# Moving weight block sums, range tests, the verdict and the last products of a gated-recurrence-plus-ELU-layer kernel

## The chip, the cores and the metric

The program runs on one core of one Trainium2 chip. The metric is the device time of one execution in microseconds. Five engines of the core matter: TensorE (PE in the profile), VectorE (DVE), ScalarE (ACT), GpSimd (POOL) and SyncE (SP), which here only issues DMAs. Each engine takes its own instructions strictly in the order in which the program lists them, and waits at an instruction until what it needs is there.

## The reference

```python
# attention block: q, k, v, a_re, a_im are (4, 8, 768, 48), float32
mag = np.sqrt(a_re * a_re + a_im * a_im)
scale = np.minimum(mag, 0.999) / (mag + 1e-06)
a_re_n, a_im_n = (a_re * scale, a_im * scale)
for t in range(S):
    ar, ai = (a_re_n[:, :, t, :, None], a_im_n[:, :, t, :, None])
    new_re = ar * S_re - ai * S_im
    new_im = ar * S_im + ai * S_re
    kv = np.einsum('bhd,bhe->bhde', k[:, :, t], v[:, :, t])
    S_re, S_im = (new_re + kv, new_im)
    y[:, :, t] = np.einsum('bhd,bhde->bhe', q[:, :, t], S_re)
# bridge: (B,H,S,D) -> (B*S, H*D) = (3072, 384) = x
h = x @ w_in                                  # (384, 2048)
g = np.where(h > 0.0, h, np.exp(np.minimum(h, 0.0)) - 1.0)
out = g @ w_out                               # (2048, 384)
```

A complex gated linear recurrence runs over 768 steps for 32 heads; its output is the input of a two-layer network with an ELU between the layers. The two weight matrices arrive as float64 and are read by the kernel as pairs of 32-bit words.

## The kernel before

**Units.** The work is cut into `NU = 12` units. A unit is 128 time steps of two batches (256 rows of the network). Two chains of batches alternate, so unit `u` hands its state and its phase to unit `u + 2`. Each unit has an attention half and a layer half.

**The attention half** works with logarithms and angles of the gates instead of stepping through time. The functions that matter here, with their lines, are: `squares` and `joined` (L709, L710, L716), `logarithms` and `powers` (L735 to L747), `lengths` (L772, reads tile `e` and is the last to do so), `ratios` (L759, L760), `slopes` (L780, the last reader of tile `w` before the carry), `angles` (L815), `carried` (L826), `turned` (matmul L837, then L842 and L845 on VectorE), `waves` (L973 to L977), `scaled` (L982 on GpSimd for k, L992 on VectorE for q) and `gated` (L1003). `carried` adds the phase that unit `u - 2` ended with to row 0 of the angles; `carry_back` (L820, a DMA on GpSimd's queue) fetches that row from DRAM into row 0 of a tile that is free by then, and `carry_on` (L862) has stored it there. `turned`'s matmul sums the angles over time, so it cannot start before `carried`. `noted` (L796, L799) reduces the gates to their least and greatest values and is the last reader of the tiles `ar` and `ai`, which have one buffer each. `states`, `scored` and `valued` (L1064 to L1145) form the attention products, and `quartered` (L889) the sums of logarithms. `seam` (L1190, six small DMAs on GpSimd's queue) moves parts of the result into the layer's input `x`.

**The layer half** of units 0 to 2 is plain (`hidden`, L1210 to L1221). From unit 3 on the first layer is a block scheme with fewer products: `mixed` (L1410) and `mixed_rest` (L1430) form sums of input blocks, and `mult` (L1450) multiplies 20 of them, in the order `ORDER = 8, 1, 6, 3, 9, 7, 5, 0, 2, 14, 12, ...`, with 20 weight blocks into five PSUM banks; `kept` (ACT, L1463) and `joint` (DVE, L1466) combine the banks, `low` (L1471, L1472) and `whole_of` (L1475) do the ELU. The second layer is a block scheme too: `folded` (DVE, L1297) prepares operands, and `product` (L1319) makes seven products P1 to P7, each in two halves `h`. When a product's second half is there, `done` inside `product` combines it (L1331, L1332, L1341 on DVE, L1339 on ACT) into an output tile `o`, which has two buffers, and issues the DMA to DRAM.

**Weight block sums.** The blocks that the schemes multiply with are sums and differences of the weights. They are made once, in place or in spare tiles, by `summed_in` (L1398, L1400; 21 of them in the list `SUMS`, each 128x512) and `combined` (L1278; eight of them, 128x768), while unit 2's plain layer still runs. Unit 3 is the first that needs them.

**Range tests.** The fast path is valid only for weights and gates in a certain range. `test_fetch` (L666, L669) loads one of `NR = 48` pieces of the raw weights into one buffer (the last quarter of `spare[1]`), `test` (L680) reduces it on VectorE. There is one such buffer, so a fetch waits for the test before it. `verdict` (L1483 to L1502) combines all of this into the flag `needs` with a matmul (L1499); at the end every engine reads the flag and skips a slow general path.

**The order** of everything is written out by hand. `first` lists the opening; after it, `put(at, fn, ...)` gives each step a place in slots, 16 slots to a unit (one unit takes about 50 us in the trace), and all steps are issued in the order of these places:

```python
    for n in range(len(SUMS)):
        put(37 + 0.6 * n if n < 11 else 45.4 + 0.6 * (n - 11), summed_in, n)
    ...
    for m in range(NR):
        put(54 + 2.5 * m, test_fetch, m)
        put(56 + 2.5 * m, test)
    put(NU * SLOTS, verdict)
```

The layer of unit `u` has its `mult`s at `16 (u - 2) + 36` and its products at `+ 44`. So between slots 45 and 53 lie, together, unit 2's products, unit 4's gates with `carried(4)` at 48.6, and the sums that unit 3's `mult`s from slot 52 on will read.

Of the kernel before, what the change touches and what calls it, by code (L numbers as in the profile page):

```python
# [505 lines left out]
def kernel(  # L506
# [179 lines left out]
    def flat(t):  # L686
        return t.rearrange("p n h d -> p (n h d)")
# [5 lines left out]
    def new(tag, bufs=1, shape=None):  # L693
        return sb.tile(shape or [C, NB, H, D], FP32, tag=tag, bufs=bufs, name=tag)
# [122 lines left out]
    def carry_back(u):  # L817

        if u in carry and u > 3:
            nc.gpsimd.dma_start(out=flat(nat[u]["w"])[0:1], in_=carry[u])  # L820

    def carried(u):

        if u in carry:
            row = nat[u]["th"][0:1].rearrange("p n h d -> p (n h d)")
            nc.vector.scalar_tensor_tensor(  # L826
                out=row, in0=carry[u] if u < 4 else flat(nat[u]["w"])[0:1], scalar=float(2 * np.pi), in1=row, op0=ALU.mult,
                op1=ALU.add,
            )

# [468 lines left out]
    def product(u, k, h):  # L1299

        x = nat[u]
        bank, n, first = {
            1: (0, 0, True), 2: (0, 0, False), 6: (0, 1, False), 5: (1, 0, True),
            7: (1, 1, False), 3: (0, 0, True), 4: (2, 0, True),
        }[k]
        if first and h == 0 and k != 3:
            x["p", bank] = work([C, 2, HN], "mlp")
        to = x["p", bank][:, n]
        a = {
            1: lambda: X(u, h, 0, 0), 2: lambda: X(u, h, 0, 1), 3: lambda: S_of(u, 4, h),  # L1310
            4: lambda: X(u, h, 1, 1), 5: lambda: S_of(u, 1, h), 6: lambda: S_of(u, 2, h),
            7: lambda: S_of(u, 3, h),
        }[k]()
        if k < 4:
            b = Y(*((0, 0), (1, 0), (1, 1))[k - 1])[:, ts(h, P // 2)]
        else:
            b = T_of({4: 4, 5: 1, 6: 2, 7: 3}[k], h)
        for m in range(P // 2):
            nc.tensor.matmul(  # L1319
                to, lhsT=a[:, m], rhs=b[:, m], start=(first and h == 0 and m == 0), stop=False,  # L1320
                skip_group_check=True,
            )
        if h == 0 or k in (4, 5):
            return
        if k == 1:
            x["u"] = new("ee", 2, [C, 2, GT])
            nc.scalar.copy(out=x["u"][:, 0, 0:HN], in_=to)
            return
        u2, u4 = (x["u"][:, n, 0:HN] for n in range(2))
        if k == 6:  # L1330
            nc.vector.tensor_tensor(out=u2, in0=to, in1=u2, op=ALU.add)  # L1331
            nc.vector.tensor_tensor(out=u4, in0=x["p", 1][:, 0], in1=u2, op=ALU.add)  # L1332
            return
        seq, at = where(u)

        def done(i, n, a, *sums):
            o = new("o", 2, [C, HN])
            if not sums:
                nc.scalar.copy(out=o, in_=a)  # L1339
            for b, op in sums:  # L1340
                nc.vector.tensor_tensor(out=o, in0=a, in1=b, op=op)  # L1341
                a = o
            nc.sync.dma_start(out=out[ds((seq + i) * S + at, C), ts(n, HN)], in_=o)

        if k == 7:
            done(1, 1, to, (u4, ALU.add))
            done(1, 0, to, (u2, ALU.add), (x["p", 2][:, 0], ALU.subtract))
        elif k == 2:
            done(0, 0, to)
        else:  # L1350
            done(0, 1, to, (u4, ALU.add))
# [13 lines left out]

    def A(r, k):

        if r == "e":
            return spare[0][:, ts(k, 4 * C)] if k < 4 else (
                more[:, k - 4] if k < 7 else spare[1][:, ds(8 * C, 4 * C)]  # L1370
            )
        h, j = ROLES[r]
        return w_in[:, k].rearrange("p (h m j f) -> p h j m f", h=2, j=2, f=C)[:, h, j]

    def four(t):
        return t.rearrange("p (m f) -> p m f", f=C) if len(t.shape) == 2 else t
# [11 lines left out]
        (17, (0, 1), PLUS, (2, 1)), (15, (0, 2), MINUS, (0, 0)), (12, 15, NEITHER, 17),  # L1388
        (17, 17, PLUS, (1, 1)), (17, 17, MINUS, 16), (2, (1, 1), MINUS, 12),
        (13, (1, 0), MINUS, 2), (11, (1, 0), MINUS, 10),  # L1390
    ] + SUMS[11:]

    def summed_in(n):

# [49 lines left out]
    def mult(u, p):  # L1444

        x = nat[u]
        c = next(c for c in BANKS if p in BANKS[c])
        a = four(A(*IN_OF[p]))
        for m in range(4):
            nc.tensor.matmul(  # L1450
                x["c" + c][:, ts(m, C)], lhsT=a[:, m], rhs=x["mix"][p],
                start=(p == BANKS[c][0] and m == 0), stop=False, skip_group_check=True,
            )
# [26 lines left out]
    def verdict():  # L1480

        ones, fit = value(1.0, "ones"), seen[:, 0 : NU + NR]
        nc.vector.tensor_tensor(  # L1483
            out=off[:, :, 0], in0=off[:, :, 0], in1=off[:, :, 1], op=ALU.add
        )
        nc.vector.tensor_scalar(
            out=least, in0=least, scalar1=LEAST_RE, scalar2=None, op0=ALU.is_ge
        )
        nc.vector.scalar_tensor_tensor(
            out=least, in0=most, scalar=LEAST_RE, in1=least, op0=ALU.is_le, op1=ALU.mult  # L1490
        )
        nc.vector.tensor_scalar(
            out=least[:, 0:OFF], in0=off[:, :, 0], scalar1=0.0, scalar2=None, op0=ALU.is_le
        )
        nc.vector.tensor_scalar(
            out=smallest, in0=smallest, scalar1=LEAST_HI, scalar2=None, op0=ALU.is_ge
        )
        t = work([1, NU + NR])
        nc.tensor.matmul(t, lhsT=ones, rhs=fit, start=True, stop=True)  # L1499
        n = cst.tile([1, 1], FP32, name="n")  # L1500
        nc.vector.tensor_reduce(out=n, in_=t, axis=mybir.AxisListType.X, op=ALU.add)
        nc.vector.tensor_scalar(  # L1502
            out=needs, in0=n, scalar1=C * (NU + NR) - 0.5, scalar2=None, op0=ALU.is_lt
        )
# [57 lines left out]
    def decays_of(u, *at):  # L1562
        fns = squares, joined, logarithms, powers, lengths, ratios, slopes, noted, angles, carried
        if u > 3:
            put(at[6] + 0.3, carry_back, u)
        put(at[0], begun, u)
        for x, fn in zip(at, fns):
            put(x, fn, u)
# [60 lines left out]
    def layer_of(u, at_h, at_p):  # L1629
# [5 lines left out]
        else:  # L1635
# [24 lines left out]
            put(at_h + 0.4 * 17.6, folded, u, 0, (3, 1))  # L1660
            put(at_h + 0.4 * 22, folded, u, 1, (3, 1))
        ks = [(k, h) for k in (1, 4, 2, 5, 6, 7, 3) for h in range(2)]
        step = 8 / len(ks)
        for m, (k, h) in enumerate(ks):
            put(at_p + m * step, product, u, k, h)
# [4 lines left out]
    for u in range(2, NU):  # L1670
        r = (u - 2) * SLOTS
        put(r + (8 if u == PAIRED else 4.5 if u == PAIRED + 3 else 1.5), load_a, u)
        put(r + 8, load_v, u)
        put(r + 8, load_qk, u)
        if u == 2:
            decays_of(u, 16, 16, 17, 17, 18.4, 19.5, 19.6, 22.7, 19.8, 19.8)
            gates_of(u, 20.4, 21.6, 22.1, 22.4, 22.4, 22.6)
        else:
            sq = (r + 7.2, r + 9.6) if u < PAIRED + 4 else (r + 5.08, r + 6)
            noting = r + (15.7 if u != PAIRED + 2 else 20.3)  # L1680
            decays_of(u, *sq, r + 12.8, r + 13.2, r + 13.4, r + 13.5, r + 14.9, noting, r + 15.52, r + 16.6)
            gates_of(u, r + 15, r + 17.2, r + 17.4, r + 18.6, r + 18)
            put(r + 18.7, gated, u, None, ("q",))
            put(r + 18.8, gated, u, None, ("k",))
            if u > PAIRED + 1:
                put(r + (19.45 if u < PAIRED + 4 else 21.1), table, "exp_and_others", u)
                put(r + 15.5, table, "trig_and_small", u)
            if u > PAIRED + 1:
                put(r + 16.8, scaled, u, "k", None)
        if u > PAIRED:  # L1690
            for n in range(NB):
                put(r + 22 + 2 * n, transposed, u, "q", n)
                put(r + 23 + 2.3 * n, transposed, u, "k", n)
            at = r + (31.3 if u + 1 < NU else 30.6)
            put(r + 28.2, scored, u)
            put(at, valued, u)
            put(at, seam, u)
            put(r + 34.45, mixed, u)
            put(r + 34.75, mixed_rest, u)
        layer_of(u, r + 36, r + 44)  # L1700
    for n in range(len(SUMS)):
        put(37 + 0.6 * n if n < 11 else 45.4 + 0.6 * (n - 11), summed_in, n)
    for m, x in enumerate(((1, 0), (2, 0), (1, 1), (4, 0), (2, 1), (4, 1), (3, 0), (3, 1))):
        put(37.2 + m * 0.6 if m < 6 else 40 + m, combined, *x)
    for m in range(NR):
        put(54 + 2.5 * m, test_fetch, m)
        put(56 + 2.5 * m, test)
    put(NU * SLOTS, verdict)
    items = [(fn, tuple(args)) for fn, *args in first]
    items += [x[2:] for x in sorted(plan, key=lambda x: x[:2]) if x[2:] not in items]  # L1710
    for fn, args in items:
# [37 lines left out]
```

## Time and profile before

| | us |
|---|---|
| median of 3 runs | 679.25 (678.58 to 681.2) |
| the profiled execution's own time | 677.98 |
| its span, first to last instruction | 676.2 |
| TensorE busy | 642.4 (95%) |
| VectorE busy | 502.3 (74%) |
| ScalarE busy | 419.1 (62%) |
| GpSimd busy | 157.8 (23%) |
| mean granted TensorE clock | 0.986 of full speed |

The page of the profile gives busy shares per engine and in 40 slices of 16.9 us. The list of waits says which engine waited for which, in us in total, times and longest. The timeline shows the instructions of one engine in order, with start, duration, and in brackets how long the engine stood idle before and what ended that. The 1.8 us between the span and the execution's own time are start and end outside the instructions.

### The profile page before, as it was taken

Reading aid. Unit: us, or ns where it says so; the run is one execution under the profiler, and the core shown is the slowest. Engines: PE = TensorE matmul, PEld = TensorE weight load, DVE = VectorE, ACT = ScalarE, POOL = GpSimd, SP = SyncE. Lnnn points to the kernel's source line nnn. Section 1 sums busy time; section 2 is a strip of 40 time slices with the busy share of each in tenths; the row PEclk is TensorE's granted clock in tenths of the full one; section 3 lists DMA queues with packets and bytes.
Section 4 is the critical chain, followed back from the end, with each engine's and each line's share of the span. In section 5 each row is a group of like instructions: output and inputs, shape, how many; then the busy total and the mean of one; then the engine's idle time right before and its main releaser. Section 6 shows DMA issues by size and latency. Waiting matters only on the chain.

```text
span 676.2 us, 17220 instructions
## 1 busy us (share of the span) xinstructions
PE 642.4 (95%) x7236; PEld 581.7 (86%) x7236; DVE 502.3 (74%) x800; ACT 419.1 (62%) x684; POOL 157.8 (23%) x200
## 2 busy tenths in 40 slices
PE   8899899999997999999999999999999999999995
PEld 6777785577896998998998998998998998999994
DVE  5889999957759678778778778778678777664481
ACT  6875455865854577677677677667677667571350
POOL 2000000122123313503503503504503503402000
PEclk9799999999998999999999999999999999999998
DMA  9995755531900452352441722441642351210000
GB/s 168 175 159 99 144 173 164 82 72 20 153 3 14 93 91 67 77 116 57 102 88 40 147 58 72 104 87 43 116 86 68 75 116 31 66 33 13 18 7 24
DMA packets 151443, 56.12 MB, mean 83 GB/s; under 512 B 129684, under 2 KB 143164, under 8 KB 151356
## 3 DMA queue, kind: packets, MB, share of 16 engines
q1 hardware_dynamic: 147616, 53.58, 39.1%
q0 software_dynamic: 3520, 1.20, 1.8%
q8 instruction: 59, 0.97, 0.6%
q14 instruction: 28, 0.23, 0.1%
q10 hardware_dynamic: 220, 0.14, 0.1%
HBM read 48.91 MB, written 4.80 MB: 79 GB/s over the span
## 4 chain that ended last, share of the span: by engine, by line
PE 53%; DVE 11%; ACT 9%; issue 4%; DMA 2%; SPq 0%; DVEq 0%; ACTq 0%
PE mlp L1319 18%; PE mlp L1450 9%; PE y L1450 6%; PE w L1023 4%; PE mlp L1210 3%; PE w L1064 3%; PE y L1109 3%; DVE g L1466 2%; PE w L837 2%; PE y L1136 2%; DVE g L1475 2%; PE mlp L1235 2%; ACT L735 2%; ACT n L746 1%; DVE g L1297 1%
## 5 line engine op out<-in xcount | busy, mean ns | idle before, releaser
L1319 PE MATMUL mlp<-w_out,g 128*128 128x192 f32 x640 | 113.3, 331 | 1.8 <-DVE ee L1332 1.8
L1319 PEld LDWEIGHTS mlp<-w_out,g 128*128 128x128 f32 x640 | 105.9, 192 | 5.5 <-DVE ee L1332 2.4
L1081 POOL TENSOR_TENSOR S<-S,T 128x384 f32<-128x384 f32 x36 | 33.6, 932 | 178.3 <-DVE S L1079 178.3
L1210 PE MATMUL mlp<-x,w_in 128*128 128x256 f32 x288 | 65.1, 381 | 2.7 <-DVE g L1221 2.4
L1210 PEld LDWEIGHTS mlp<-x,w_in 128*128 128x128 f32 x288 | 53.8, 190 | 11.3 <-DVE g L1221 2.8
L1297 DVE TENSOR_TENSOR g<-g 128x512 f32<-128x512 f32 x80 | 57.7, 731 | 5.0 <-PE mlp L1319 3.8
L1466 DVE TENSOR_TENSOR g<-g,mlp 128x512 f32<-128x512 f32 x45 | 30.7, 683 | 38.2 <-PE mlp L1450 23.9
L1450 PE MATMUL mlp<-x,w_in 128*128 128x128 f32 x432 | 57.2, 275 | 0.0
L1319 PE MATMUL mlp<-w,g 128*128 128x192 f32 x320 | 54.7, 329 | 0.0
L1475 DVE SCALAR_TENSOR_TENSOR g<-ee,g 128x512 f32<-128x512 f32 x63 | 44.1, 700 | 12.2 <-ACT ee L1472 11.9
L1450 PEld LDWEIGHTS mlp<-x,w_in 128*128 128x128 f32 x432 | 52.6, 192 | 0.0
L1319 PEld LDWEIGHTS mlp<-w,g 128*128 128x128 f32 x320 | 51.8, 190 | 0.7
L1471 ACT ACTIVATE ee<-g 128x512 f32<-128x512 f32 x63 | 39.5, 627 | 19.5 <-DVE g L1466 19.3
L1463 ACT COPY g<-mlp 128x512 f32<-128x512 f32 x36 | 21.2, 588 | 43.4 <-PE mlp L1450 43.2
L1472 ACT ACTIVATE ee<-ee 128x512 f32<-128x512 f32 x72 | 45.4, 631 | 2.3
L1190 POOL DMA_DIRECT2D x<-y x62 | 30.1, 493 | 59.4 <-ACT y L1126 37.5
L973 ACT ACTIVATE cs<-n 128x768 f32<-128x768 f32 (+1 forms) x14 | 10.5, 750 | 43.1 <-DVE n L845 43.1
L1024 ACT COPY qt<-w 128x512 f32<-128x512 f32 x48 | 25.8, 589 | 16.0 <-PE w L1023 15.9
L904 ACT ACTIVATE n<-w 64x384 f32<-64x384 f32 (+1 forms) x60 | 28.1, 486 | 8.9 <-PE w L889 8.3
L1450 PE MATMUL y<-x,w_in 128*128 128x128 f32 x216 | 29.3, 278 | 4.0 <-ACT g L1463 4.0
L1450 PEld LDWEIGHTS y<-x,w_in 128*128 128x128 f32 x216 | 26.2, 192 | 4.9 <-ACT g L1463 4.8
L1219 ACT ACTIVATE ee<-mlp 128x512 f32<-128x512 f32 x24 | 14.3, 595 | 25.6 <-PE mlp L1210 16.8
(218 smaller groups left out, 1436.8 us busy)
## 6 DMA issues: line engine op xcount, KB each, us to landing
w<-in_moe_w_out_dram SPq DMA_DIRECT2D x8, 768.0 KB, 4.4
g<-in_moe_w_in_dram SPq DMA_DIRECT2D x24, 256.0 KB, 3.0
g<-in_moe_w_out_dram SPq DMA_DIRECT2D x24, 256.0 KB, 2.9
w<-in_moe_w_in_dram SPq DMA_DIRECT2D x16, 288.0 KB, 5.7
vn<-in_v_dram SPq DMA_DIRECT2D x24, 192.0 KB, 3.9
out_dram<-o SPq DMA_DIRECT2D x48, 96.0 KB, 2.2
ar<-in_a_re_dram SPq DMA_DIRECT2D x22, 192.0 KB, 3.6
ai<-in_a_im_dram SPq DMA_DIRECT2D x22, 192.0 KB, 4.3
```

The costliest lines, as they stand in the source:

```text
L904: nc.scalar.activation(out=flat(x[key][to, n : n + 1]), in_=t[of], func=AF.Exp, scale=sign)
L1023: nc.tensor.transpose(t[:, h], of, ident)
L1081: eng.tensor_tensor(out=new_s, in0=new_s, in1=wide, op=ALU.mult)
L1190: eng.dma_start(out=x["x"][ds(j * HP + D, G), i], in_=x["y"][ds(j * HP + i * G, G)])
L1210: nc.tensor.matmul(t[:, e], lhsT=w_in[:, i, ts(f + e, C)], rhs=x["x"][:, i], start=(i == 0), stop=(i == NI - 1),)
L1297: nc.vector.tensor_tensor(out=S_of(u, k, h), in0=a, in1=b, op=op)
L1319: nc.tensor.matmul(to, lhsT=a[:, m], rhs=b[:, m], start=(first and h == 0 and m == 0), stop=False, skip_group_check=True,)
L1450: nc.tensor.matmul(x["c" + c][:, ts(m, C)], lhsT=a[:, m], rhs=x["mix"][p], start=(p == BANKS[c][0] and m == 0), stop=False, skip_group_che ...
L1466: nc.vector.tensor_tensor(out=part(u, to), in0=part(u, a), in1=part(u, b), op=op)
L1471: nc.scalar.activation(out=e, in_=part(u, of), func=AF.Relu, scale=-1.0)
L1472: nc.scalar.activation(out=e, in_=e, func=AF.Exp, scale=-1.0)
L1475: nc.vector.scalar_tensor_tensor(out=part(u, to), in0=nat[u]["e", to], scalar=-1.0, in1=part(u, of), op0=ALU.add, op1=ALU.max,)
```

## The change

Six edits, all of them in where steps stand or which buffer they use:

1. The 21 sums get places one by one. The first 11 stay. Of the other ten, one (index 20) stays ahead of `carried(4)` and nine go behind it, from slot 49.3 to 59.5, among unit 3's layer. A new 22nd sum makes block 6 a second time, in the still unused test buffer, ahead of the carry (slot 45); unit 3's `mult` of block 6 reads that copy, so that the sum in place (index 19) can come after unit 3's layer. Two `combined` steps move from slots 46 and 47 to 40.8 and 41.4.
2. `carry_back` goes from after `slopes` to after `lengths`, into tile `e` instead of tile `w`.
3. `noted(4)` moves from slot 52.3 to 49.6.
4. The 48 tests stand at six fixed places in each unit instead of every 2.5 slots, and each fetch comes right behind the test before it.
5. `verdict` moves 7.5 slots forward and is cut in two; the part that reads the matmul's result, `pronounced`, comes 2.5 slots later.
6. In the last two units the last four product halves go (3, h0), (7, h0), (7, h1), (3, h1) instead of (7, h0), (7, h1), (3, h0), (3, h1). The last unit's four output tiles are taken from the ring `S` (eight buffers) instead of the ring `o` (two).

```diff
     def carry_back(u):
         if u in carry and u > 3:
-            nc.gpsimd.dma_start(out=flat(nat[u]["w"])[0:1], in_=carry[u])
+            nc.gpsimd.dma_start(out=flat(nat[u]["e"])[0:1], in_=carry[u])
...
-                out=row, in0=carry[u] if u < 4 else flat(nat[u]["w"])[0:1], scalar=float(2 * np.pi), in1=row, op0=ALU.mult,
+                out=row, in0=carry[u] if u < 4 else flat(nat[u]["e"])[0:1], scalar=float(2 * np.pi), in1=row, op0=ALU.mult,
...
         def done(i, n, a, *sums):
-            o = new("o", 2, [C, HN])
+            if u < NU - 1:
+                o = new("o", 2, [C, HN])
+            else:
+                o = flat(new("S", 8, [C, 1, H, D]))[:, 0:HN]
...
     def A(r, k):
+        if r == "t":
+            return spare[1][:, ds(12 * C, 4 * C)]
...
-    ] + SUMS[11:]
+    ] + SUMS[11:] + [(("t", 0), (1, 1), MINUS, 5)]
...
-        a = four(A(*IN_OF[p]))
+        a = four(A(*(("t", 0) if p == 6 and u == PAIRED + 1 else IN_OF[p])))
...
-        t = work([1, NU + NR])
+        nat[0]["fit"] = t = work([1, NU + NR])
         nc.tensor.matmul(t, lhsT=ones, rhs=fit, start=True, stop=True)
+    def pronounced():
+        t = nat[0]["fit"]
...
         if u > 3:
-            put(at[6] + 0.3, carry_back, u)
+            put(at[4] + 0.05, carry_back, u)
...
         ks = [(k, h) for k in (1, 4, 2, 5, 6, 7, 3) for h in range(2)]
+        if u > NU - 3:
+            ks[-4:] = (3, 0), (7, 0), (7, 1), (3, 1)
...
-            noting = r + (15.7 if u != PAIRED + 2 else 20.3)
+            noting = r + (15.7 if u != PAIRED + 2 else 17.6)
...
-    for n in range(len(SUMS)):
-        put(37 + 0.6 * n if n < 11 else 45.4 + 0.6 * (n - 11), summed_in, n)
+    for n in range(11):
+        put(37 + 0.6 * n, summed_in, n)
+    for n, at in (
+        (21, 45), (20, 46.5), (11, 49.3), (12, 49.4), (13, 49.5), (16, 50.2), (14, 54.3),
+        (15, 55.1), (17, 56), (18, 57), (19, 59.5),
+    ):
+        put(at, summed_in, n)
...
-        put(37.2 + m * 0.6 if m < 6 else 40 + m, combined, *x)
+        put(37.2 + m * 0.6, combined, *x)
+    clear = [SLOTS * n + x for n in range(3, NU) for x in (0.55, 5.2, 7.35, 9.7, 12.3, 14.2)]
+    clear = [x for x in clear if x > 57]
     for m in range(NR):
-        put(54 + 2.5 * m, test_fetch, m)
-        put(56 + 2.5 * m, test)
-    put(NU * SLOTS, verdict)
+        put(clear[m - 1] + 0.01 if m else 55, test_fetch, m)
+        put(clear[m], test)
+    put(NU * SLOTS - 7.5, verdict)
+    put(NU * SLOTS - 5, pronounced)
```

More of the change, by code (lines that the diff above doesn't have):

```diff
@@ L1700 @@
         layer_of(u, r + 36, r + 44)
-    for n in range(len(SUMS)):
-        put(37 + 0.6 * n if n < 11 else 45.4 + 0.6 * (n - 11), summed_in, n)
+    for n in range(11):
[5 more added lines that the diff above has]
+        put(at, summed_in, n)
     for m, x in enumerate(((1, 0), (2, 0), (1, 1), (4, 0), (2, 1), (4, 1), (3, 0), (3, 1))):
-        put(37.2 + m * 0.6 if m < 6 else 40 + m, combined, *x)
+        put(37.2 + m * 0.6, combined, *x)
+    clear = [SLOTS * n + x for n in range(3, NU) for x in (0.55, 5.2, 7.35, 9.7, 12.3, 14.2)]
+    clear = [x for x in clear if x > 57]
     for m in range(NR):
-        put(54 + 2.5 * m, test_fetch, m)
-        put(56 + 2.5 * m, test)
-    put(NU * SLOTS, verdict)
+        put(clear[m - 1] + 0.01 if m else 55, test_fetch, m)
+        put(clear[m], test)
+    assert clear[NR - 1] < NU * SLOTS - 8
+    put(NU * SLOTS - 7.5, verdict)
+    put(NU * SLOTS - 5, pronounced)
     items = [(fn, tuple(args)) for fn, *args in first]
```

## The prediction

> **What bounds the kernel now.** First the page's slices (40 of 16.9 us each, digits are tenths):
>
> ```profile
> PE   8899899999997999999999999999999999999995
> ...
> DVE  5889999957759678778778778778678777664481
> ...
> PEclk9799999999998999999999999999999999999998
> ```
>
> TensorE is the bound: nine tenths or more in nearly every slice. The exception after the opening is the 13th slice (203 to 220 us), where TensorE falls to 7, VectorE stands at 9 and the clock then dips. So the question is what TensorE waits for. The waits, longest first:
>
> ```profile
> PE w L837 <- DVE n L826: 4.3, 1, 4.3
> PE y L1450 <- ACT g L1463: 4.0, 4, 1.8
> ...
> PE w L889 <- DVE n L772: 2.0, 8, 0.3
> PE mlp L1319 <- DVE ee L1332: 1.8, 2, 0.9
> ```
>
> One wait of 4.3 us for the carry, four of 4.0 us together in the `mult`s, eight of a quarter microsecond (0.25 each, paced by ScalarE's table loads; no edit touches them). The timeline shows the long one, and beside it the same steps four units' worth later, undisturbed:
>
> ```profile
> 215.00 2.90 PE L837 MATMUL w<-n,sum_turns 128*128 128x384 f32 x4 [4.31 <-DVE n L826]
> 217.69 6.90 PE L1319 MATMUL mlp<-w_out,g 128*128 128x192 f32 x32
> ...
> 371.74 1.53 PE L837 MATMUL w<-n,sum_turns 128*128 128x384 f32 x4
> 373.11 5.36 PE L1319 MATMUL mlp<-w_out,g 128*128 128x192 f32 x32
> ```
>
> TensorE idles 4.31 us, and then the same matmuls take nearly twice as long: from 215.00 to the first `mult` at 224.43 are 9.43 us, from 371.74 to 378.31 6.57 us. That is another 2.86 us. Why `carried` (L826) was late, and what it met:
>
> ```profile
> 212.24 2.62 DVE L826 SCALAR_TENSOR_TENSOR n<-n 1x768 f32<-1x768 f32 x1
> ...
> 212.22 1.81 POOL L982 TENSOR_TENSOR k<-k,n 128x768 f32<-128x768 f32 x1
> ...
> 370.65 0.95 DVE L826 SCALAR_TENSOR_TENSOR n<-n 1x768 f32<-1x768 f32 x1 [0.35 <-ACT n L815]
> ```
>
> VectorE is busy without a gap from 201.48, with six sums and two `combined` between `lengths` and `carried`, and reaches L826 at 212.24, though ScalarE had its angles ready at 209.65. There it starts 13 ns after GpSimd's L982 and takes 2.62 us instead of 0.95.
>
> The `mult` waits come from tests that stand too close to the one before; the single buffer makes each wait out a whole transfer:
>
> ```profile
> 588.52 0.42 DVE L680 TENSOR_REDUCE seen<-g 128x1 f32<-128x256 f32 x1 [3.45 <-DMA g<-in_moe_w_out_dram]
> ...
> 592.36 1.16 PE L1450 MATMUL y<-x,w_in 128*128 128x128 f32 x8 [1.11 <-ACT g L1463]
> ...
> 669.93 0.36 DVE L1341 TENSOR_TENSOR o<-mlp,ee 128x192 f32<-128x192 f32 x1 [2.35 <-DMA out_dram<-o]
> ```
>
> VectorE stands at the test, so `joint` is late, so ScalarE's `kept` is late, so TensorE waits. The last line is the tail: the final output tile waits for an earlier one's DMA, since `o` has two buffers.
>
> [...] the clock stands at one half for 6.83 us from 213.97 (6.83/2 = 3.4 us lost, 2.86 of them before the first `mult`), and no later gap (1.78 us at most) does it. [...] 2.62 us is L982's rest, 1.80, and L826's own 0.95 less overlap. [...] the tests' transfers here, from SP, take 2.6 us at least, 2.9 to 3.0 in the median and 4.8 at most, which I use.
>
> **The change, part by part.** Signs are of time; negative is a gain.
>
> *Sums and carry (edits 1 and 2).* VectorE's costs from start to start in the trace: 0.60 us for a 128x512 sum, 0.87 for a 128x768 step. In the changed order only two sums (the copy of block 6, which stands in VectorE's 3.55 us idle before L772, and one more) remain ahead. From 201.48: L772, L759, L760 (0.87 + 0.98 + 0.87), one L1297, one sum, L780, two L1297 end at about 207.5. L826 then waits for ScalarE alone, until 209.65, as it does at 370.65. GpSimd: `seam`'s six DMAs cannot start before ScalarE's L1180 ends (207.5) and take 2.88 us, so L982 starts at about 210.4, with L826 under way. `carry_back`'s DMA, now after L772 at 202.4, has 7 us for a landing of 2.1. So L837 starts at 210.7, where TensorE gets there: **-4.31, and -2.86 of half clock.** The two `combined` (2 x 0.87) fall into VectorE's idle stretches of 1.3 to 1.6 us ahead of L1221 around 186: 0.
>
> *What is late next.* The four sums placed at 49.3 to 50.2 and the two reductions of `noted(4)` stand between L845 and `done`'s L1341: 4 x 0.60 + 2 x 0.87 = 4.1 us. In the undisturbed unit VectorE has 1.04 us idle there. So L1341 comes 3.0 us later than the undisturbed place: at 217.9 instead of 214.9. The first `mult` needs a PSUM bank that the second L1341 frees (0.62 later, 218.5), where TensorE would be ready at 217.3: 1.3 us. The second `mult` needs `halves`, the second L1410, 1.8 us after the first L1341: another 0.3. The sixth needs the bank read by the fourth L1341, 6.15 us after the first, 224.0, where TensorE would be at 223.3: 0.7. **+2.3.** [...] The sums at 54.3 to 57 (4 x 0.60) lie where VectorE waits 2 to 3 us for TensorE in each unit: 0[...]. The last sum stands in the dense end of the ELU chain: 0.60, less a test that left: **+0.3.** All readers come after the sums, by more than 5 us.
>
> *`noted(4)` earlier (edit 3).* It frees `ai` sooner; SP then issues unit 5's loads behind the last output of unit 2, at about 224.5 instead of 229.8. The 1.78 us gap at 237.19 had 0.44 us of waiting for that load on ScalarE; the rest is `squares(5)` itself standing ahead of `kept`. **-0.45.**
>
> *Tests (edit 4).* 48 x 0.33 us before and after. Between tests there are now 4.1 us at least (slots 14.2 to 16.55: L780, one L1297, L796, L799, one L1297), else 6 or more, against transfers of 2.9 to 3.0. SP has nothing before these fetches that waits. The loads of v, q, k move 6 us behind a fetch; they are read 25 us later. The three other `mult` gaps go: **-0.15, -0.99, -1.11.**
>
> *Verdict (edit 5).* Five small steps (0.74 us from 657.29 to 658.03) fall into 2.07 us of idle VectorE at 641; the matmul's 0.2 us only moves. L1501 and L1502 (0.31) now stand in the chain that product P4 waits for (0.53 us at 651.51): **+0.3.**
>
> *Last products (edit 6).* P7 waits for L1332, twice, 0.91 us; P3 instead waits only for L1331, which ends 0.38 earlier, and covers L1332: **-0.76.** In the tail the last L1341 follows the last matmul (669.13) at 669.2 instead of 669.93: **-0.7.**
>
> Sum: -7.17 + 2.3 + 0.3 - 0.45 - 2.25 + 0.3 - 0.76 - 0.7 = **-8.4 us.** Against the profiled 677.98 that is 669.6. The median is 1.3 above that execution, so I forecast 679.25 - 8.4 = **670.8.**
>
> **Bounds.** The wait ahead of `mult` is not in the trace before: between 0 (then 668.5) and 3.0 plus a half-clock stretch of 3.4 (then 674.9); I take the reckoned 2.3. The half clock may not be lost in every timed run[...]: up to +2.9. The rest of the 1.78 gap may go: -1.3.
>
> **Rivals.** *A. The queue is shifted, not removed.* The sums hold up the `mult`s for 3 us and the clock falls again: 670.8 + 0.7 + 3.4 = 674.9. For it: VectorE is as full there as before the carry. Against: three short gaps[...]. *B. No half clock in the timed runs, and the fixed tests wait as the old ones did:* 670.8 + 2.9 + 2.25 = 676.0, no difference. Against: 4.1 us of distance is more than the median landing. *C, slower: the test ahead of the carry.* In units 5 to 11 a test stands right ahead of `carried`, its fetch 3.7 us earlier. If the piece lands later than that plus 0.4 us, L826 falls behind GpSimd's L982[...], and L837 is late by some 2.5 us in each unit: 7 x 2.5 = 17.5, 670.8 + 17.5 = 688. It decides from a landing of 4.1 us; for slower by over 0.5% ((8.4 + 3.4)/2.5) five of the seven must fail. For it: one transfer took 4.8. Against: the median is 3.0, and the w_out pieces never took over 3.1. *D. No wait ahead of `mult`, all else as reckoned:* 668.5.
>
> **Chances.** Forecast 0.63 (its own range 668.5 to 673), A 0.17, B 0.09, C 0.04, D 0.07. A measurement here can tell about 0.5%, 3.4 us, from no change: below 675.9 is faster. Faster 0.63 + 0.17 + 0.07 = 0.87, same 0.09, slower 0.04. Range 667.0 to 675.5; B and C are left out.
>
> **What would show it.** L826 0.95 us long after ScalarE's L815, L837 with no idle before it, no half clock near 214; then short gaps ahead of L1450 at about 217 to 224 waiting for L1341 and L1410, 2.3 us in all; no L680 waiting for a DMA; about 1.3 us left at the `y` `mult` behind `squares(5)`; 0.5 us ahead of P3; the last L1341 right behind the last matmul. A half clock near 220, or L826 late in later units, would make it wrong.

## The result and the profile after

| | before | changed |
|---|---|---|
| median | 679.4 us (678.58 to 681.2, 4 runs) | 671.36 us (669.23 to 671.93, 4 runs) |
| the profiled execution's own time | 677.98 | 669.23 |
| its span | 676.2 | 667.1 |
| TensorE busy | 642.4 | 639.6 |

The ratio is 0.9872 (95% interval 0.9843 to 0.9902): 1.3% faster. A later repeat of the same kernel gave 670.48 us and 0.9877 (0.9829 to 0.9925). The forecast was 670.8 us.

The page's slices of the changed kernel (40 of 16.7 us each, tenths):

```profile
PE   8899899999999899999999999999999999999995
...
DVE  5889999968777788678678768768768768765481
...
PEclk9799999999999999999999999999999999999999
```

The hole in the 13th slice is gone, on TensorE and in the clock alike, and VectorE's 9 there has become a 7. A 14th slice of 8 has appeared instead. (The functions' lines have moved by a few: L1341 is now L1344, L1410 L1415, L1450 L1455, L1463 L1468, L1466 L1471, L1398 and L1400 are L1403 and L1405. L826, L837, L982, L1319 and L680 are as before.) TensorE's waits, from the list of waits:

```profile
PE mlp L1455 <- DVE o L1344: 1.7, 2, 1.2
...
PE y L1455 <- ACT g L1468: 1.4, 1, 1.4
...
PE mlp L1319 <- DVE ee L1331: 1.0, 2, 0.5
```

L837 waits for `carried` no more, one `y` mult waits for `kept` instead of four, and a wait that was not there before has come: mults for `done`'s L1344. The timeline around unit 4's carry and unit 3's first mults (start, duration, engine, and in brackets the idle time before and what ended it):

```profile
209.58 0.95 DVE L826 SCALAR_TENSOR_TENSOR n<-n 1x768 f32<-1x768 f32 x1 [2.11 <-ACT n L815]
...
210.57 1.82 POOL L982 TENSOR_TENSOR k<-k,n 128x768 f32<-128x768 f32 x1
...
210.67 1.53 PE L837 MATMUL w<-n,sum_turns 128*128 128x384 f32 x4
...
218.63 1.16 PE L1455 MATMUL mlp<-x,g 128*128 128x128 f32 x8 [1.23 <-DVE o L1344]
...
219.94 0.97 PEld L1455 LDWEIGHTS mlp<-halves,g 128*128 128x128 f32 x8 [0.34 <-DVE halves L1415]
219.94 1.16 PE L1455 MATMUL mlp<-halves,g 128*128 128x128 f32 x8
...
224.27 1.16 PE L1455 MATMUL mlp<-x,w_in 128*128 128x128 f32 x8 [0.45 <-DVE o L1344]
...
232.30 1.16 PE L1455 MATMUL y<-x,w_in 128*128 128x128 f32 x8 [1.39 <-ACT g L1468]
```

VectorE now idles 2.11 us ahead of L826 and takes 0.95 us for it; L982 comes afterwards; L837 has no idle time before it. Three short gaps follow (1.23, 0.34 for `halves` at 219.94, 0.45), the middle one read ahead of the weight load (PEld), since the matmuls themselves stood for 0.15 us only; and 1.39 us remain at the `y` mult behind `squares(5)`.

**Where the 9.07 us of span went.** For each TensorE step one subtracts its start in the trace before from its start in the trace after. Where that difference jumps, time was gained or lost:

| step of the prediction | reckoned | measured |
|---|---|---|
| start of the compared stretch | 0 | -0.11 |
| wait of L837 for the carry | -4.31 | -4.22 |
| half clock up to the first mult | -2.86 | -2.86 |
| new waits ahead of mults | +2.3 | +2.69 (idle 1.23, 0.34, 0.45; most of the rest: mults that had waited took 1.16 us, not 1.06) |
| the `y` mult at 237 (noted earlier) | -0.45 | -0.39 |
| last sum in the ELU chain | +0.3 | +0.28 |
| three test waits | -2.25 | -3.02 |
| verdict and P4 | +0.3 | +0.31 up to P4, then -0.40, the matmul having left the end |
| P3 ahead of P7, twice | -0.76 | -0.78 |
| after the last matmul | -0.7 | -0.56 |
| sum | -8.4 | -9.06 |

### The profile page after: what moved, and what is told of

Read it like the earlier page. It is cut to its first block, busy times and chain, and to the rows that moved or that the text cites. A ratio compares the mean times of both kernels' runs of the same rounds, so it can differ in the third digit from the quotient of the medians.

```text
span 667.1 us, 17231 instructions
## 1 busy us (share of the span) xinstructions
PE 639.6 (96%) x7236; PEld 579.6 (87%) x7236; DVE 503.6 (75%) x801; ACT 419.2 (63%) x684; POOL 154.4 (23%) x200
## 4 chain that ended last, share of the span: by engine, by line
PE 44%; DVE 10%; ACT 8%; issue 3%; DMA 1%; SPq 0%; ACTq 0%; DVEq 0%
PE mlp L1319 18%; PE mlp L1455 10%; PE y L1455 5%; DVE g L1471 3%; PE w L1023 3%; DVE g L1480 3%; PE y L1109 2%; ACT ee L1477 2%; ACT ee L1476 2%; PE w L1064 2%; PE w L837 2%; DVE g L1297 1%; ACT L735 1%; DVE n L772 1%; ACT n L746 1%
## 5 line engine op out<-in xcount | busy, mean ns | idle before, releaser
L1319 PE MATMUL mlp<-w_out,g 128*128 128x192 f32 x640 | 111.8, 328 | 1.0 <-DVE ee L1331 1.0
L1319 PEld LDWEIGHTS mlp<-w_out,g 128*128 128x128 f32 x640 | 104.2, 190 | 4.4 <-DVE ee L1331 1.6
L1081 POOL TENSOR_TENSOR S<-S,T 128x384 f32<-128x384 f32 x36 | 30.9, 857 | 175.5 <-DVE S L1079 175.5
L1471 DVE TENSOR_TENSOR g<-g,mlp 128x512 f32<-128x512 f32 x45 | 30.7, 682 | 40.1 <-ACT qt L1024 28.7
L1297 DVE TENSOR_TENSOR g<-g 128x512 f32<-128x512 f32 x80 | 54.4, 695 | 5.0 <-PE mlp L1319 3.8
L1455 PE MATMUL mlp<-x,w_in 128*128 128x128 f32 x424 | 56.2, 275 | 0.4 <-DVE o L1344 0.4
L1480 DVE SCALAR_TENSOR_TENSOR g<-ee,g 128x512 f32<-128x512 f32 x63 | 47.6, 755 | 11.1 <-ACT ee L1477 11.0
L1319 PE MATMUL mlp<-w,g 128*128 128x192 f32 x320 | 54.5, 329 | 0.0
L1319 PEld LDWEIGHTS mlp<-w,g 128*128 128x128 f32 x320 | 51.8, 190 | 0.6
L1455 PEld LDWEIGHTS mlp<-x,w_in 128*128 128x128 f32 x424 | 51.6, 192 | 0.8 <-DVE o L1344 0.6
L1476 ACT ACTIVATE ee<-g 128x512 f32<-128x512 f32 x63 | 39.5, 627 | 17.2 <-DVE g L1471 16.7
L1468 ACT COPY g<-mlp 128x512 f32<-128x512 f32 x36 | 21.1, 586 | 44.0 <-PE mlp L1455 43.7
L1455 PE MATMUL mlp<-x,g 128*128 128x128 f32 x224 | 29.7, 275 | 1.2 <-DVE o L1344 1.2
L1455 PE MATMUL y<-x,w_in 128*128 128x128 f32 x216 | 29.0, 277 | 1.4 <-ACT g L1468 1.4
```

Source lines behind the costliest of these rows:

```text
L1081: eng.tensor_tensor(out=new_s, in0=new_s, in1=wide, op=ALU.mult)
L1297: nc.vector.tensor_tensor(out=S_of(u, k, h), in0=a, in1=b, op=op)
L1319: nc.tensor.matmul(to, lhsT=a[:, m], rhs=b[:, m], start=(first and h == 0 and m == 0), stop=False, skip_group_check=True,)
L1455: nc.tensor.matmul(x["c" + c][:, ts(m, C)], lhsT=a[:, m], rhs=x["mix"][p], start=(p == BANKS[c][0] and m == 0), stop=False, skip_group_che ...
L1471: nc.vector.tensor_tensor(out=part(u, to), in0=part(u, a), in1=part(u, b), op=op)
L1476: nc.scalar.activation(out=e, in_=part(u, of), func=AF.Relu, scale=-1.0)
```

## Experiments

**How they are read.** Up to the start of unit 2's product P6 (195.7 us in the changed kernel's trace) TensorE runs the same instructions in the same order in all these kernels; on VectorE the two `combined` of edit 1 stand elsewhere in some of them. This opening took from 195.2 to 201.5 us. It holds half clock, and not the same stretches of it in every execution (6.83 us in each of the two traces above; one to three windows more in the first four experiments, by the expectation for `after_again`). So small effects are read from that point on in the traces; "from 195.7 on" means this. The timed ratios contain the opening's scatter: their intervals for `sums_back`, `sums_back_k_later`, `sums_back_carry_new`, `tests_back` and `tail_back` all overlap the changed kernel's, so the timed runs alone don't show these differences. Each share below comes from one trace of each kernel. Edits 3 and 5 were not taken back alone; their shares stand only in the table above.

**The changed kernel again** (`after_again`).

> The changed kernel once more, as the measure for the runs beside it. From 195.7 us on (the start of unit 2's product of P6, before which the edits change nothing) the trace should repeat within 0.3 us; the opening before it may differ by several us, as it did in the last four runs (3.4 to 5.8 us with one to three more windows of half clock).

Measured: 670.48 us; every TensorE start from 195.7 on agrees within 0.1 us, behind an opening 1.47 us longer. So a shift of a few tenths in one trace is readable.

**The sums back ahead of the carry** (`sums_back`).

```diff
-    for n in range(11):
-        put(37 + 0.6 * n, summed_in, n)
-    for n, at in (
-        (21, 45), (20, 46.5), (11, 49.3), (12, 49.4), (13, 49.5), (16, 50.2), (14, 54.3),
-        (15, 55.1), (17, 56), (18, 57), (19, 59.5),
-    ):
-        put(at, summed_in, n)
+    for n in range(len(SUMS) - 1):
+        put(37 + 0.6 * n if n < 11 else 45.4 + 0.6 * (n - 11), summed_in, n)
...
-        put(37.2 + m * 0.6, combined, *x)
+        put(37.2 + m * 0.6 if m < 6 else 40 + m, combined, *x)
...
-            put(at[4] + 0.05, carry_back, u)
+            put(at[6] + 0.3, carry_back, u)
```

The row goes back into tile `w`, and unit 3's mult of block 6 reads the block in place, without the copy.

> Compared with the changed kernel (profiled span 667.1, timed median 671.4). Theory: the sums queued on VectorE ahead of the carry were the cost, so with the ten sums, the two combined and carry_back at their old places L837 again waits 4.3 us for L826, the clock falls to one half for 6.8 us (2.9 us more before the first mult), while the three waits ahead of the first mults (1.23 + 0.34 + 0.45) and the 0.3 us of the last sum in the ELU chain go: 7.2 - 2.3 = +4.9 us, a span of about 672.0. Rival 1: the gain of the sums is only shifted into the waits ahead of mult and the timed runs lose the clock again anyway: +2 us or less. Rival 2: the carry was late for another reason than the queue, such as its DMA: L826 then shows idle time before it that ends with that DMA.

Measured: 674.24 us, ratio to before 0.9897 (0.9863 to 0.9931). Timeline:

```profile
215.49 1.81 POOL L982 TENSOR_TENSOR k<-k,n 128x768 f32<-128x768 f32 x1
215.51 2.61 DVE L826 SCALAR_TENSOR_TENSOR n<-n 1x768 f32<-1x768 f32 x1
...
218.27 2.90 PE L837 MATMUL w<-n,sum_turns 128*128 128x384 f32 x4 [4.31 <-DVE n L826]
```

The old picture is back: L826 meets L982, L837 waits 4.31 us and takes 2.90 us at half clock. From 195.7 on the kernel is 4.0 us slower, not 4.9: the half clock cost 2.3 us this time instead of 2.9. In the trace that is twice what rival 1 allowed. No idle time ended by a DMA stands before L826, so rival 2 falls.

**Is it the queue or the overlap with L982?** (`sums_back_k_later`)

```diff
-                put(r + 16.8, scaled, u, "k", None)
+                put(r + (17.6 if u == PAIRED + 2 else 16.8), scaled, u, "k", None)
```

> As sums_back, but unit 4's scaled k (L982 on GpSimd) is issued behind the turns instead of ahead of them. Theory [...]: L826 starts at about the same time but takes 0.95 us instead of 2.62, the gap ahead of L837 is about 2.6 us, no clock of one half follows it: 1.7 + 2.9 = 4.6 us less than sums_back, span about 667.5. Rival (the clock falls with any gap of this kind): 1.7 us less only. Rival [...]: L826 still takes 2.6 us and nothing changes.

Measured: 674.09 us, ratio 0.988 (0.9845 to 0.9916). Timeline:

```profile
215.61 0.94 DVE L826 SCALAR_TENSOR_TENSOR n<-n 1x768 f32<-1x768 f32 x1
...
216.69 1.53 PE L837 MATMUL w<-n,sum_turns 128*128 128x384 f32 x4 [2.64 <-DVE n L826]
...
220.71 1.83 POOL L982 TENSOR_TENSOR k<-k,n 128x768 f32<-128x768 f32 x1
...
221.56 2.15 DVE L1403 TENSOR_TENSOR w_in<-w_in,g 128x512 f32<-128x512 f32 x2
...
224.29 1.16 PE L1455 MATMUL mlp<-x,g 128*128 128x128 f32 x8 [0.87 <-DVE o L1344]
```

The first half of the theory holds: L826 takes 0.94 us, the gap is 2.64 and the clock does not fall. But only 1.6 us are won against `sums_back`, not 4.6. That is the first rival's number, though not for its reason, since the clock did not fall. L982 now overlaps two sums in front of L1344, which take 2.15 us instead of the 1.28 they took in `sums_back`, and the mults wait there (0.87 and 1.05 us). The queue accounts for 2.6 of the 4.3 us, the overlap of L982 and L826 for 1.7.

**Edit 2 alone in the old order** (`sums_back_carry_new`): `sums_back` with `carry_back` at its new place.

> As sums_back (all sums and combined at their old places), but carry_back stays at its new place after lengths, in tile e. Theory: its old place made it wait for L780, and GpSimd's six seam transfers and L982 stood behind it on the queue, so that L982 met L826 (215.49 against 215.51 in sums_back). Now seam can start about 1.7 us earlier, L982 is over when L826 comes, the gap ahead of L837 is 2.7 us instead of 4.3 and no clock of one half follows: -1.6 - 2.1 us, of which the waits ahead of the first mults may take back up to 2. Net -2 to -3.7 against sums_back from 195.7 us on. Rival (edit 2 had no part in the gain): the gap stays 4.3 us and nothing changes.

Measured: 675.08 us, ratio 0.9921 (0.9887 to 0.9955). The theory fell. Timeline:

```profile
210.66 3.29 POOL L982 TENSOR_TENSOR k<-k,n 128x768 f32<-128x768 f32 x1
...
212.21 2.55 DVE L826 SCALAR_TENSOR_TENSOR n<-n 1x768 f32<-1x768 f32 x1
```

L982 did start 1.55 us ahead of L826, but it takes 3.29 us instead of 1.8: the three VectorE steps that ran meanwhile kept their 0.68 to 0.69 us. So the two met all the same, and L826 took 2.55 us. The gap is 4.16 us, and from 195.7 on the kernel is 3.9 us slower than the changed one, as `sums_back` is. **And without the sums** (`carry_old`, the three `carry_back` lines alone undone):

> The changed kernel with carry_back alone at its old place (after slopes, in tile w). In sums_back_carry_new the new place brought nothing while the sums stood ahead of the carry. Theory (nor does it without them: L780 ends at about 206.3, ahead of ScalarE's L1180 at 207.4, so L820 holds up neither seam nor L982, and it lands 1 us before L826): TensorE's starts from 195.7 us on agree with the changed kernel within 0.1 us. Rival (L820 now lands late, or pushes L982 onto L826): L826 shows a wait for a DMA or takes 2 us or more, L837 is late by 1 us or more in unit 4 and by some tenths in the later ones.

Measured: 668.46 us (one run); from 195.7 on TensorE's starts are within 0.15 us of the changed kernel's. `carried` waits for ScalarE alone, as in the changed kernel:

```profile
209.22 0.94 DVE L826 SCALAR_TENSOR_TENSOR n<-n 1x768 f32<-1x768 f32 x1 [2.12 <-ACT n L815]
```

In these traces edit 2 was worth nothing, in either order; edit 1 carried the whole gain at the carry.

**The tests back to every 2.5 slots** (`tests_back`).

```diff
-        put(clear[m - 1] + 0.01 if m else 55, test_fetch, m)
-        put(clear[m], test)
+        put(54 + 2.5 * m, test_fetch, m)
+        put(56 + 2.5 * m, test)
```

> The changed kernel with fetches and tests every 2.5 slots as before. Theory: second tests of close pairs wait for their transfer on VectorE, and three waits of y mults for ScalarE's kept come back (0.15 + 0.99 + 1.11): +2.25 us, span about 669.4, three or so L680 with idle time ended by a DMA. Rival (those waits had another cause, such as unit 4's late start that shifted everything): no L680 wait reaches TensorE, +0.

Measured: 675.34 us, ratio 0.99 (0.9856 to 0.9944); from 195.7 on 2.85 us slower. VectorE stands 11.4 us for seven fetches, and the timeline's `y` mults have their waits again (1.02 us twice). One of them, with the test ahead of it:

```profile
486.48 0.42 DVE L680 TENSOR_REDUCE seen<-g 128x1 f32<-128x256 f32 x1 [3.20 <-DMA g<-in_moe_w_out_dram]
...
491.12 1.16 PE L1455 MATMUL y<-x,w_in 128*128 128x128 f32 x8 [1.02 <-ACT g L1468]
```

Besides, 0.3 us that the changed kernel had won near 350 us, where the kernel before had L1064 wait 0.32 us for L1079, are lost again. So that gain, which the forecast had not seen, belongs to the tests.

**Edit 6 undone** (`tail_back`).

```diff
-            if u < NU - 1:
-                o = new("o", 2, [C, HN])
-            else:
-                o = flat(new("S", 8, [C, 1, H, D]))[:, 0:HN]
+            o = new("o", 2, [C, HN])
...
-        if u > NU - 3:
-            ks[-4:] = (3, 0), (7, 0), (7, 1), (3, 1)
```

> The changed kernel with the old order of the last products and with o as the last unit's output tiles. Theory: P7 waits 0.91 instead of 0.52 us twice (+0.8) and the last output tile waits for an earlier one's DMA (+0.6): +1.4 us, span about 668.5. Rival (the tail's end is set by the DMA that was issued last, whatever the tile): +0.8 only.

Measured: 671.53 us, ratio 0.9856 (0.9808 to 0.9903). From 195.7 on the last products come 0.44 and 0.39 us later, and from the last matmul to the end are 7.0 us instead of 6.5: +1.4 us in the trace, as expected. The last `done`, here and in the changed kernel:

```profile
668.02 0.36 DVE L1341 TENSOR_TENSOR o<-mlp,ee 128x192 f32<-128x192 f32 x1 [2.19 <-DMA out_dram<-o]
...
660.66 0.36 DVE L1344 TENSOR_TENSOR S<-mlp,ee 128x192 f32<-128x192 f32 x1 [0.29 <-PE mlp L1319]
```

The timed median does not show it (the ratio is even 0.0016 below the changed kernel's).

**A test too close to the carry** (`test_close`).

```diff
-    clear = [SLOTS * n + x for n in range(3, NU) for x in (0.55, 5.2, 7.35, 9.7, 12.3, 14.2)]
+    clear = [SLOTS * n + x for n in range(3, NU) for x in (0.55, 5.2, 7.35, 9.7, 12.3, 15.8)]
```

> The changed kernel with the test of slot 14.2 moved to 15.8, so that the fetch of the test right ahead of the carry is issued some 0.9 us before that test instead of 4.1. Number of tests unchanged. Theory (rival C of the prediction: the carry has 0.34 us to spare[...]): VectorE stands about 2 us at the test, L826 starts at L982's end, L837 is about 3 us late in seven units: +20 us, more if the clock falls in some of them. Rival (VectorE's later idle stretches of 1 us and more absorb it): L837 late by 2 us at most and part of it won back ahead of mult, under +10 us.

Measured: 701.54 us (2 runs), ratio to before 1.0327 (1.0246 to 1.0408), 31 us over the changed kernel. One of the seven units in the timeline:

```profile
375.35 1.82 POOL L982 TENSOR_TENSOR k<-k,n 128x768 f32<-128x768 f32 x1
375.61 0.42 DVE L680 TENSOR_REDUCE seen<-g 128x1 f32<-128x256 f32 x1 [2.22 <-DMA g<-in_moe_w_in_dram]
375.94 2.04 DVE L826 SCALAR_TENSOR_TENSOR n<-n 1x768 f32<-1x768 f32 x1
...
378.14 2.26 PE L837 MATMUL w<-n,sum_turns 128*128 128x384 f32 x3 [3.08 <-DVE n L826]
```

VectorE stands 2.22 us at the test, L826 then falls behind L982 (2.04 instead of 0.95 us), and L837 waits 3.08 us, as rival C had it. In all seven units the gap was 3.06 to 3.08 us and the clock fell too (L837's four matmuls took 1.92 to 2.90 us instead of 1.53). Of the 33.5 us in the trace 20.8 are gaps and 12.7 follow them at half clock. One test of each unit, moved by 1.6 slots, costs nearly four times what the whole change gained.

**Which gap lowers the clock?** (`dose_up`, `dose_down`)

```diff
+            for wide in {
+                5: (256, 768, 768), 6: 3 * (768,), 7: (256, 768, 768, 768),
+                8: (256, 256, 768, 768, 768), 9: 4 * (768,),
+                10: (256, 768, 768, 768, 768), 11: 5 * (768,),
+            }.get(u, ()):
+                nc.vector.tensor_reduce(
+                    out=least[:, u : u + 1], in_=flat(nat[u]["ar"])[:, 0:wide],
+                    axis=mybir.AxisListType.X, op=ALU.min
+                )
             nc.vector.scalar_tensor_tensor(
...
-                put(r + 16.8, scaled, u, "k", None)
+                put(r + (16.8 if u == PAIRED + 2 else 17.6), scaled, u, "k", None)
```

> The changed kernel with added reductions on VectorE right ahead of L826 in units 5 to 11 (2.07, 2.6, 2.9, 3.3, 3.5, 3.8 and 4.35 us of work; they repeat a reduction of the gates and change no value), and L982 of these units issued behind the turns[...]. L837 should wait 0.34 us less than the added work: 1.7, 2.3, 2.6, 2.9, 3.1, 3.5 and 4.0 us. Theory 1 [...]: a clock of one half in units 10 and 11 only. Theory 2 [...]: falls from about 3.0 us on, in some units and not in others[...].

> As dose_up with the doses in the opposite order (4.35 us in unit 5 to 2.07 us in unit 11)[...]. Theory 1: a clock of one half in units 5 and 6 only. Theory 2: the same lengths as in dose_up need not give the same answer between 2.6 and 4 us.

Measured: 708.16 and 706.94 us (one run each). Gaps of 1.96, 2.49, 2.95, 3.40, 3.48, 3.93 and 4.47 us in one, 4.47, 3.93, 3.48, 3.40, 2.95, 3.08 and 3.08 in the other (in the last two units no carry is stored that could hold back L982, so that it met L826 there, which took 2.05 us in the last one of `dose_down`). The clock fell after all fourteen: L837's four matmuls took 2.27 to 2.90 us instead of 1.53. Theory 1 falls, since the two longest gaps were not the only ones. Theory 2 missed as well: it had the falls begin at about 3.0 us, and some gaps spared. Yet the length alone did not decide either, as the list of windows shows (stretch, its length, busy time of TensorE's matmuls with their number, then the other engines; behind the parentheses the granted clock). First `sums_back_k_later`, whose gap of 2.64 us left the clock alone:

```profile
212.56:215.97 3.41, 1.49 (x10) 1.20 (x8) 3.41 (x7) 0.47 (x1) 2.96 (x7) 1.00 0.11 27
215.97:219.39 3.42, 2.70 (x13) 2.19 (x14) 3.32 (x8) 0.00 (x0) 0.00 (x0) 1.00 0.02 5
```

and `dose_up`, where a gap of 1.96 us brought it down:

```profile
267.27:270.68 3.41, 1.45 (x10) 1.19 (x9) 3.34 (x6) 0.33 (x1) 1.64 (x4) 1.00 0.33 102
270.68:274.09 3.41, 3.41 (x7) 2.20 (x8) 2.11 (x6) 0.00 (x0) 0.00 (x0) 0.50 1.17 206
```

The clock stayed at 1.00 through the longer gap and stood at 0.50 for 3.41 us behind the shorter one. TensorE's busy time in the first stretch of each, 1.49 against 1.45 us, lies too close together to tell the two apart; the last section has the other cases.

**A better version** (`fill`, then `fill_more`).

```diff
-            noting = r + (15.7 if u != PAIRED + 2 else 17.6)
+            noting = r + 15.7
-        (21, 45), (20, 46.5), (11, 49.3), (12, 49.4), (13, 49.5), (16, 50.2), (14, 54.3),
-        (15, 55.1), (17, 56), (18, 57), (19, 59.5),
+        (21, 45), (20, 46.5), (11, 45.3), (12, 45.32), (13, 45.34), (16, 50.2), (14, 54.3),
+        (15, 55.1), (17, 56), (18, 57), (19, 59.5),
```

> The changed kernel with three sums (11, 12, 13) moved into VectorE's 2.3 us of idle time ahead of unit 4's L772, and noted(4) into the 2.1 us ahead of L826, where the other units have it. Theory (the 3.5 us of work between L845 and L1344 are what the first mults wait for, and both idle stretches have room: 1.8 and 1.74 us): L826 stays where it is, the waits of 1.23, 0.34 and 0.45 us go: -2.0 us from 195.7 us on. Rival (VectorE is full ahead of the carry): L826 late and behind L982, +1 to +3 us and perhaps a window of half clock.

Measured: 668.03 us, ratio to before 0.9846 (0.9796 to 0.9895). From 195.7 on 2.9 us less than the changed kernel, more than the 2.0 expected; the timed medians differ by 2.4 us, with overlapping runs (666.74 to 671.6 against 669.63 to 672.41). `fill_more` has in addition:

```diff
-            sq = (r + 7.2, r + 9.6) if u < PAIRED + 4 else (r + 5.08, r + 6)
+            sq = (r + (7.2 if u != PAIRED + 3 else 7.85), r + 9.6) if u < PAIRED + 4 else (r + 5.08, r + 6)
-        (15, 55.1), (17, 56), (18, 57), (19, 59.5),
+        (15, 55.1), (17, 56), (18, 57), (19, 56.2),
```

> As fill, and squares(5) moved behind the two kept that it stood ahead of (slot 55.85 instead of 55.2), and the last sum (19) moved from the ELU chain to slot 56.2, where VectorE idles 4.4 us. Theory: the y mult's wait of 1.39 us and the 0.28 us ahead of L1064 and L1319 at 248 also go: -3.7 us against the changed kernel from 195.7 us on, a timed median about 3.5 us below it. Rival (the y mult waits for kept because its own bank is late, not because of squares): -2.3.

Measured: 665.74 us, ratio to before 0.9796 (0.9748 to 0.9844); on the same chip the changed kernel had 670.48. From 195.7 on it is 4.7 us less, more than the 3.7 expected: each removed wait gave back some tenths beside its idle time. Timeline:

```profile
211.86 0.95 DVE L826 SCALAR_TENSOR_TENSOR n<-n 1x768 f32<-1x768 f32 x1 [0.40 <-ACT n L815]
...
219.52 1.05 PE L1455 MATMUL mlp<-x,g 128*128 128x128 f32 x8
...
230.24 1.10 PE L1455 MATMUL y<-x,w_in 128*128 128x128 f32 x8
```

L826 has 0.40 us of idle time left instead of 2.11, so both fillings fit; neither the first mult nor the `y` mult waits any more. Its six runs (663.62 to 667.18) are all below the six of the changed kernel on this chip, so it beats both kernels.

## Why the prediction was right, point by point

The forecast of 670.8 us came within 0.6 us of the median, 671.36. That closeness is in part luck: the opening alone differs by up to 6 us between executions, and in the trace the gain was 9.07 us where 8.4 were reckoned. What holds is the list of steps, most of them right to some tenths.

- **Sums and carry: right, and for the reason given.** Idle 4.31 us gone, L826 behind ScalarE's L815 alone, L982 a microsecond later. `sums_back` reversed it. The prediction gave edits 1 and 2 one sum; `sums_back_carry_new` and `carry_old` show that edit 2 had no share.
- **Half clock: right in size (2.86), but not bound to a gap of that length.** The gap of 4.31 us lowered the clock in both traces that have it (before and `sums_back`), but so did 3.08 us in `test_close` and 1.96 us in `dose_up`. Rival B's half, that timed runs might not lose the clock, is unlikely for this gap, since each gap of 2.95 us or more ahead of L837 lowered the clock in the traces; the timed runs don't tell. The prediction also read 3.4 us of loss from the half clock's 6.83 us and put 2.86 of it ahead of the first mult. But the half clock ended at 220.80, ahead of that mult, so 2.86 was all of it: TensorE was idle for the first 1.03 us of the stretch.
- **What is late next: right.** Reckoned 1.3, 0.3 and 0.7 us; idle 1.23, 0.34 and 0.45. Full clock behind these gaps was the author's estimate, and it held: the granted clock is 1.00 throughout (with two of the gaps in one stretch of 3.42 us, TensorE was still busy 2.31 us of it). A wait of 3 us, the upper bound that was named, could have lowered the clock, as 3.06 to 3.08 us did in all seven units of `test_close`: rival A was nearer than the text said. `fill` took the wait away by giving the 3.5 us of work another place.
- **noted(4) and the last sum: right** (-0.39 and +0.28). `fill_more` removed both remainders.
- **Tests: right in kind, 0.8 us too small.** The forecast counted the idle time of the three `y` mults alone. A mult that had waited also took 1.16 instead of 1.06 us in these traces, and the tests had held up an L1064 near 354 us by 0.3 us; `tests_back` returned 2.85 of the 3.02 us. L680 waits for no DMA in the changed kernel, so the second half of rival B fell.
- **Verdict: too dear.** P4's wait grew by 0.09 us, not 0.3: the 0.31 us of small steps lie partly in idle time. The matmul does move 0.3 us forward and leaves the end.
- **Last products and tail: right** (-0.78 and -0.56 against -0.76 and -0.7); `tail_back` returned 1.4 us.
- **Rival A** did not come about: the gaps were 1.23, 0.34 and 0.45 us, and the clock stayed at 1.00. **Rival C** did not come about at a distance of 4.1 us between tests, but `test_close` shows it to be real: 3.0 us of gap for each unit where 2.5 were reckoned, and the clock on top. **Rival D** needs the wait ahead of mult to vanish, and it was there.

## What to carry to other kernels

When work is taken out of a full stretch of one engine, ask at once who waits behind the place where it is put down: here 2.7 of 7.1 us came back as waits two steps later, and the same work placed into idle stretches that the trace had shown all along (2.3 us ahead of L772, 2.1 us ahead of L826) cost nothing that the trace shows. A long wait has several parts, and an operation that is only moved can lengthen others at its new place, as L982 did with two sums in `sums_back_k_later` (2.15 us instead of 1.28); subtracting the starts of the bound engine's steps in two traces shows which part went where, to a tenth of a microsecond. Steps that may have to wait for a transfer do not belong right ahead of the one step that the bound engine is waiting for: in `test_close` that cost 3.06 to 3.08 us of waiting in each of seven units.

## What the runs showed of the hardware that was not expected

**The length of a gap alone did not decide about the clock.** Ahead of L837 the gaps of 1.96 and 2.49 us (`dose_up`) and all those from 2.95 to 4.47 us (`dose_up`, `dose_down`, `test_close`, `sums_back`, `sums_back_carry_new` and before) were followed by half clock; the gap of 2.64 us in `sums_back_k_later` was not, nor was the one of 1.78 us at 237.19 in the trace before. TensorE's busy time in the 3.41 us ahead of a fall does not sort the cases either. It was 0.13 us ahead of the fall at 213.97 in the trace before, 0.52 ahead of the one at 377.96 in `test_close` and 1.45 ahead of the one at 270.68 in `dose_up`; but in the opening it was 2.20 us ahead of the fall at 19.41 (before) and 2.35 ahead of the one at 19.70 (changed kernel), while a stretch with 1.49 us in `sums_back_k_later` and one with 1.63 us in the trace before (234.45 to 237.86) were followed by full clock. What decides is open. The half clock lasted 6.83 us in the trace before and 3.41 us behind the shortest gap of `dose_up`. It cost 2.86 us in the former, 2.3 in `sums_back`, and 12.7 us in the seven units of `test_close`, about 1.8 each.

**An overlap cost both engines.** L982 took 1.81 us where it met L826 in `sums_back`, and L826 2.61 us instead of 0.95. In `sums_back_carry_new` (one place in one trace) L982 took 3.29 us, 1.48 more, with VectorE's steps following each other without a pause at 0.68 to 0.69 us each, and L826 behind them took 2.55 us. What the two engines wait for there is not shown. An earlier start was no protection here.
